# Attention with a soft mixture of experts: weights and output stored tile by tile

## The chip, the cores and the metric

The kernel runs on one core of one Trainium2 chip. The metric is the time on the device in microseconds (us), the median of several runs. What the host does before the launch and after it, such as rearranging arrays, is not in that time. The core has five engines with a queue of instructions each: PE (matmul), DVE and ACT (elementwise work and evacuation of the matmul's results from PSUM), POOL, and SP, which here issues nearly all transfers. Sixteen DMA engines move the data. A tile in SBUF has up to 128 partitions; in a transfer each partition's data is one row or several, and a row is a run of bytes that is contiguous on both sides.

## The reference

Attention over 8 batches and 8 heads with 576 positions and 64 channels, with rotary position embedding of q and k, followed by a soft mixture of 8 experts with 4 slots each. All is float32.

```python
q_rot, k_rot = (rotate(q), rotate(k))
attn = softmax(q_rot @ k_rot.T / sqrt(64))
x = (attn @ v) laid out as [B * S, H * D]        # 4608 x 512
logits = x @ phi                                  # 4608 x 32
d = softmax of logits over the 4608 rows
slot_input = d.T @ x                              # 32 x 512, 4 slots of each expert
h = relu(slot_input[e] @ w1[e])                   # w1: 8 x 512 x 1024
slot_out[e] = h @ w2[e]                           # w2: 8 x 1024 x 512
c = softmax of logits over the 32 slots
return c @ slot_out                               # 4608 x 512
```

## The kernel before, in words

*Attention* is worked through in 32 pairs of heads. For each pair, q, k and v are loaded as tiles of 128 partitions with one row of 4608 bytes each (`fetch`, L137, and `load_v`, L161): the host has already laid these arrays out tile by tile. POOL and DVE rotate them, PE forms the scores and the products with v, ACT takes the exponentials, and a few small transfers (L209, L210, L274, L286, L293) carry maxima and sums between partitions. After every four pairs a batch is complete, and its logits and its part of `slot_input` are added up. The order of all these steps on the engines is a written table of times (`WHEN`), one entry per step.

*Weights.* w1 and w2 are cut into 64 tiles of 128 partitions and 4096 bytes per partition, 32 tiles each. `load_w` (L474) loads the next tile in a fixed order, with one transfer on SP's queue (L485). A w1 tile has the shape [128, 2, 512]: partition p holds rows p and 128 + p of a block of 256 rows of one expert's w1, and 512 of its 1024 columns. A w2 tile has the shape [128, 4, 256]: four rows, and 256 of 512 columns. So in memory a w1 tile comes in rows of 2048 bytes, 256 of them, and a w2 tile in rows of 1024 bytes, 512 of them. Indices 0 to 31 of `order` are w1, the others w2; a few w1 tiles are moved back in the order, and all w1 tiles come ahead of the w2 tiles.

SBUF does not hold all 64 tiles. 24 are loaded in the course of attention (`weights`), seven more when the input buffers of attention are given up (`release_io`, `trickle`), four more in `release_stk` and one in `release_att`. Two go into the pool `wb`, and seven (`N_LEAD`, L771) and the last 19 (L869) into buffers of the first 24: each of these transfers waits until PE has used the tile that lay in its buffer. SP issues in program order, and so a load that waits holds back everything behind it.

*The expert layers* come when attention is over. `ffn1` (L781) multiplies the slots of four experts at a time with w1, in four steps of 32 matmuls (L785), with a transpose after each (L797). `ffn2_steps` (L800) multiplies with w2 for one half of the 512 output columns (`mh`), in 16 steps of 4 matmuls (L809). `gather` (L817) brings the result together for that half.

*The combination.* `combine(mh, sl, b)` (L828) does four matmuls (L837) for one output tile of [128, 4, 256], has ACT and DVE evacuate two halves (L838), and writes the tile with one transfer. For b from 0 to 7 the tile holds positions 0 to 511 of batch b (L841). For b = 8 it holds positions 512 to 575 of all eight batches, and goes in two transfers of 64 partitions (L844). There are nine tiles for each half of the columns, 18 in all, and they use seven buffers in turn. The output is a [4608, 512] array, so a tile's rows in memory are 1024 bytes long and 2048 bytes apart. The nine combinations of the first half alternate on PE with the ffn2 steps of the second (`STEPS`, L41); those of the second half follow its gather.

Output transfers stand on SP's queue behind all the weight loads, as the program issues them later.

Of the kernel before, what the change touches and what calls it, by code (L numbers as in the profile page):

```python
# [7 lines left out]
F32 = mybir.dt.float32  # L8
# [7 lines left out]
B, H, S, D = 8, 8, 576, 64  # L16
# [3 lines left out]
DM = H * D  # L20
E, SPE, FF = 8, 4, 1024
# [45 lines left out]
def attn_softmoe(ctx, tc, qk, v, phi, w1, w2, cs, ident, sel, seg, out):  # L67
    nc = tc.nc
    P = 128
# [95 lines left out]
    def bank2():  # L165
        return ps_s.tile([P, 2, 512], F32, name="s_ps")
# [307 lines left out]
    def load_w(pool, bufs, tag="w_exp"):  # L474
        n = order[len(w_tiles)]
        layer, rest = divmod(n, 4 * E)
        if layer == 0:
            grp, f, ch, x = rest // 16, rest // 8 % 2, rest // 4 % 2, rest % 4
            src = w1[4 * grp + x].rearrange("(c p) f -> p c f", p=P)[:, 2 * ch:2 * ch + 2, 512 * f:512 * f + 512]
            wt = pool.tile([P, 2, 512], F32, name=tag, bufs=bufs)  # L480
        else:
            mh, grp, fh, x = rest // 16, rest // 8 % 2, rest // 4 % 2, rest % 4
            src = w2[4 * grp + x].rearrange("(c p) m -> p c m", p=P)[:, 4 * fh:4 * fh + 4, 256 * mh:256 * mh + 256]
            wt = pool.tile([P, 4, 256], F32, name=tag, bufs=bufs)
        nc.sync.dma_start(out=wt, in_=src)  # L485
        w_tiles[n] = wt


# [7 lines left out]
    def trickle(p):  # L496
        if later:
            load_w(*later.pop(0))

    def release_stk():  # L500
        early.close()
        hx = ctx.enter_context(tc.tile_pool(name="hx", bufs=1, side="right", reuse_waits="tile"))
        extra.append(hx)
        load_w(hx, 1, "wk")
        we = ctx.enter_context(tc.tile_pool(name="we", bufs=N_WE, side="right", reuse_waits="tile"))
        for _ in range(N_WE):
            load_w(we, N_WE)
# [94 lines left out]
    for t, cc in ((1, 0), (1, 1), (0, 0), (0, 1)):  # L602
        c = half[cc]
# [12 lines left out]
    o = bank2()  # L616
# [49 lines left out]
    p = NPAIR - 1  # L666
# [11 lines left out]
    o = ps_o.tile([P, 2, 512], F32, name="o_ps")[:, 0]  # L678
# [31 lines left out]
    m, al, dt, xn = state["m"], state["al"], state["dt"], xns.pop(B - 1)  # L710
# [26 lines left out]
    o = sp[:, 1]  # L737
# [37 lines left out]

    cst, crt, _ = c_tiles[0]
    seg_sb = c_tiles[1]
    of = out.rearrange("(b s) m -> b s m", b=B)
    hts = {}

    def ffn1(grp, f):  # L781
        hp = ps_s.tile([P, 2, 512], F32, name="s_ps")
        for i in range(NP):
            for x in range(4):
                nc.tensor.matmul(hp[32 * x:32 * x + 32, 0, :], lhsT=st[:, i, SPE * (4 * grp + x):SPE * (4 * grp + x) + 32],  # L785
                                 rhs=w_tiles[16 * grp + 8 * f + 4 * (i // 2) + x][:, i % 2, :],
                                 start=(i == 0), stop=(i == NP - 1), tile_position=(0, 32 * x))
        hs = tail.tile([P, 512], F32, name="hs", bufs=2)
        nc.vector.tensor_scalar_max(out=hs, in0=hp[:, 0, :], scalar1=0.0)
        return hs  # L790
# [35 lines left out]
        return sl  # L826

    def combine(mh, sl, b):  # L828
        ms = slice(256 * mh, 256 * mh + 256)
        k = (9 * mh + b) % (N_WA + N_WB)  # L830
        ob = (wb.tile([P, 4, 256], F32, name=f"w_exp{k}") if k < N_WB else
              extra[0].tile([P, 4, 256], F32, name="w_exp", bufs=N_WA))
        for jj in range(2):
            o = ps_t.tile([P, 512], F32, name="t_ps")
            for j in (2 * jj, 2 * jj + 1):
                lhs = cst[b // 2][:, b % 2, j, :] if b < B else crt[:, 2 * j:2 * j + 2, :].rearrange("p b i -> p (b i)")
                nc.tensor.matmul(o[:, 256 * (j % 2):256 * (j % 2) + 256], lhsT=lhs, rhs=sl, start=True, stop=True)  # L837
            (nc.vector.tensor_copy if jj else nc.scalar.copy)(  # L838
                out=ob[:, 2 * jj:2 * jj + 2, :], in_=o.rearrange("p (j m) -> p j m", j=2))
        if b < B:  # L840
            nc.sync.dma_start(out=of[b, 0:512, ms].rearrange("(j p) m -> p j m", p=P), in_=ob)  # L841
        else:
            for h in range(2):
                nc.sync.dma_start(out=of[h::2, 512:576, ms].rearrange("b p m -> p b m"), in_=ob[64 * h:64 * h + 64])  # L844

    turned, split = 2, 2

# [15 lines left out]
    for grp, f in ((0, 1), (1, 0), (1, 1)):  # L863
        h = ffn1(grp, f)
# [21 lines left out]
    for b in range(B + 1):  # L886
        combine(0, sl0, b)
        if turned < NP:
            if b == LATE[0]:
                c_tr(turned)  # L890
                late_evac = c_evac(turned, True)
            elif b > LATE[0]:
                for _ in range(LATE[1]):
                    next(late_evac, None)
        for _ in range(STEPS[b]):
            next(steps, None)
# [3 lines left out]
    for b in range(B + 1):  # L900
        combine(1, sl1, b)
# [44 lines left out]
```

## Time and profile before

| What | Value |
|---|---|
| Median of 3 runs | 559.78 us (559.6 to 560.85) |
| The profiled execution | 559.26 us, span 557.3 us |
| Busy in the span | PE 518.8 us (93%), DVE 430.7 (77%), POOL 325.9 (58%), ACT 311.5 (56%) |
| Transfers | 111.31 MB in 74,618 packets, 200 GB/s on average |
| Memory | 99.93 MB read, 9.58 MB written |
| Weight tiles | 64 transfers of 512 KB |
| Output tiles | 16 transfers of 512 KB and 4 of 256 KB |

The span runs from the first to the last instruction of the profiled execution; what the execution takes beside it, 2.0 us, is not resolved. In the tables of busy time by stretch the DMA share is the sum of the packets' durations over the sixteen engines and the stretch; it can exceed 1 where packets of one engine overlap. A rate in GB/s is 10^9 bytes per second, so a weight or output tile of 512 KB has 524,288 bytes. In the chain of waits a row with DMA lasts from the issue of a transfer to its landing.

### The profile page before, as it was taken

The page shows a single profiled execution, that of the slowest core. Times are in us where ns is not written, and L with a number is a line of the kernel's source. Part 1 is how long each engine was busy: PE and PEld are TensorE (multiplying, and loading weights), DVE is VectorE, ACT ScalarE, POOL GpSimd, SP SyncE. Part 2 cuts the span into 40 slices and gives each one's busy share as a digit, 9 for nine tenths or more (in the row PEclk, how much of TensorE's full clock was granted, in tenths as well). Part 3 has the DMA queues.
Part 4 walks back from the last instruction along what each step waited for, and adds up shares of the span by engine and source line. Part 5 has one row for each costly group of instructions (what it writes and reads, how often), then busy time and mean ns, then how long its engine had stood idle before and what let it go on. Part 6 is the DMA issues. An engine that isn't in the chain of part 4 may idle for free.

```text
span 557.3 us, 25024 instructions
## 1 busy us (share of the span) xinstructions
PE 518.8 (93%) x11164; PEld 389.7 (70%) x11164; DVE 430.7 (77%) x580; ACT 311.5 (56%) x655; POOL 325.9 (58%) x324
## 2 busy tenths in 40 slices
PE   4679999999999999999999999999999999999770
PEld 2367877877787787777877887787778876635350
DVE  5779999889988998999889988997999732421350
ACT  2145666666656665666666666665666565334240
POOL 2867878876877688668786976688664111200000
PEclk9679999999999999999999999999999999999995
DMA  7254556665555565656556655565442267399997
GB/s 261 90 213 132 190 195 204 192 190 186 194 191 189 189 192 189 190 179 202 189 189 191 199 181 190 197 199 179 147 152 78 77 220 256 116 325 348 352 379 256
DMA packets 74618, 111.31 MB, mean 200 GB/s; under 512 B 11536, under 2 KB 54288, under 8 KB 74512
## 3 DMA queue, kind: packets, MB, share of 16 engines
q1 hardware_dynamic: 74498, 109.73, 60.6%
q8 instruction: 87, 1.43, 1.1%
q14 instruction: 19, 0.16, 0.1%
q10 hardware_dynamic: 14, 0.00, 0.0%
HBM read 99.93 MB, written 9.58 MB: 196 GB/s over the span
## 4 chain that ended last, share of the span: by engine, by line
PE 83%; DVE 6%; DMA 6%; ACT 1%; SPq 1%; issue 1%; DVEq 0%; ACTq 0%
PE o_ps L238 25%; PE s_ps L225 25%; PE s_ps L263 9%; PE s_ps L175 6%; PE s_ps L331 3%; DMA w_exp<-in_w 3%; PE s_ps L785 3%; PE s_ps L346 2%; DVE nm L177 2%; DMA x_in<-in_qk 2%; PE s_ps L400 1%; DVE hl L155 1%; DMA out<-w_exp 1%; PE o_ps L809 1%; DVE x_in L146 1%; PE s_ps L200 1%
## 5 line engine op out<-in xcount | busy, mean ns | idle before, releaser
L142 POOL TENSOR_TENSOR x_in<-x_in,cs_sb 128x288 f32<-128x288 f32 x248 | 256.2, 1067 | 80.2 <-DMA x_in<-in_qk 78.0
L226 ACT ACTIVATE a_t<-s_ps 128x576 f32<-128x576 f32 x288 | 179.6, 652 | 89.3 <-PE s_ps L225 88.9
L177 DVE TENSOR_REDUCE nm<-s_ps 128x2 f32<-128x576 f32 x256 | 182.9, 749 | 40.0 <-PE s_ps L175 38.3
L238 PE MATMUL o_ps<-a_t,v_in 64*64 64x288 f32 x2304 | 195.8, 408 | 0.0
L225 PE MATMUL s_ps<-hl 64*64 64x288 f16 x3456 | 167.2, 286 | 3.6 <-DVE nm L177 3.2
L225 PEld LDWEIGHTS <-hl 64*64 64x64 f16 x3456 | 125.1, 107 | 28.8 <-issue 5.4
L225 PE MATMUL s_ps<-peak,lift 64*64 64x288 f16 x1152 | 100.1, 284 | 0.3 <-issue 0.3
L238 PEld LDWEIGHTS o_ps<-a_t,v_in 64*64 64x64 f32 x2304 | 85.8, 133 | 8.2 <-issue 0.5
L175 PE MATMUL s_ps<-hl 64*64 64x288 f16 x1024 | 79.6, 291 | 3.6 <-DVE nm L177 3.6
L297 POOL TENSOR_TENSOR xt<-xt,rb 128x576 f32<-128x576 f32 x30 | 45.6, 1521 | 31.7 <-DMA rb<-r_row 24.2
L252 DVE TENSOR_TENSOR c_t<-a_t 128x1728 f32<-128x1728 f32 x32 | 62.4, 1951 | 0.0
L155 DVE TENSOR_TENSOR hl<-x_in,hl 128x1152 f16<-128x1152 f32 x32 | 60.7, 1897 | 0.5 <-ACT hl L151 0.5
L146 DVE TENSOR_TENSOR x_in<-x_in 128x1152 f32<-128x1152 f32 (+2 forms) x36 | 56.2, 1560 | 0.1
L175 PEld LDWEIGHTS <-hl 64*64 64x64 f16 x1024 | 38.3, 106 | 24.1 <-issue 14.9
L151 ACT CAST hl<-x_in 128x576 f16<-128x576 f32 (+1 forms) x66 | 40.2, 653 | 23.5 <-DVE x_in L146 21.7
L225 PEld LDWEIGHTS <-lift 64*64 64x64 f16 x1152 | 46.6, 108 | 0.7 <-issue 0.5
L337 ACT COPY xn<-s_ps 128x512 f32<-128x512 f32 x31 | 18.0, 582 | 29.2 <-PE s_ps L332 29.2
L420 POOL TENSOR_TENSOR ln<-ln,cm 128x160 f32<-128x160 f32 x7 | 14.7, 2096 | 33.3 <-DVE cm L419 33.3
L269 ACT ACTIVATE s<-s_ps,bits 128x144 f32<-128x144 f32 x32 | 12.2, 380 | 34.1 <-ACT xn L338 14.2
L263 PE MATMUL s_ps<-c_t,pick 128*32 128x144 f32 x768 | 30.0, 289 | 0.3 <-DVE c_t L252 0.2
L263 PE MATMUL s_ps<-a_t,pick 128*32 128x144 f32 x768 | 29.7, 286 | 0.0
L838 DVE COPY w_exp<-t_ps 128x512 f32<-128x512 f32 x18 | 12.3, 690 | 19.1 <-PE t_ps L837 17.5
(174 smaller groups left out, 475.4 us busy)
## 6 DMA issues: line engine op xcount, KB each, us to landing
x_in<-in_qk SPq DMA_DIRECT2D x62, 576.0 KB
w_exp<-in_w SPq DMA_DIRECT2D x63, 512.0 KB
v_in<-in_v SPq DMA_DIRECT2D x32, 576.0 KB
rb<-r_row SPq DMA_DIRECT2D x60, 144.0 KB
out<-w_exp SPq DMA_DIRECT2D x16, 512.0 KB
x_in<-in_qk SPq DMA_DIRECT2D x4, 288.0 KB
out<-w_exp SPq DMA_DIRECT2D x4, 256.0 KB
cs_sb<-in_cs SPq DMA_DIRECT2D x2, 288.0 KB
```

The costliest lines, as they stand in the source:

```text
L142: eng.tensor_tensor(out=x[:, :, c], in0=x[:, :, c], in1=cs_sb[:, :, c], op=ALU.mult)
L146: nc.vector.tensor_tensor(out=x[:, t, 0, c], in0=x[:, t, 0, c], in1=x[:, t, 1, c], op=ALU.add)
L151: nc.scalar.copy(out=halves[p][:, 1 + t, c], in_=loaded[p][:, t, 0, c])
L155: nc.vector.tensor_tensor(out=hl[:, 0:4:3], in0=x[:, :, 0], in1=hl[:, 1:3], op=ALU.subtract)
L175: nc.tensor.matmul(s[rows[c ^ h], h, 0:HC], lhsT=hl[rows[h], QH, at:at + 64], rhs=hl[rows[h], KH, half[n]], start=True, stop=True)
L177: nc.vector.tensor_reduce(out=nms[p][:, n, j:8:4], in_=s[:, :, 0:HC], axis=AX.X, op=ALU.max, negate=True)
L225: nc.tensor.matmul(s[rows[h ^ n], n, 0:HC], lhsT=lhs, rhs=rhs, start=(x == 0), stop=(x == 3))
L226: nc.scalar.activation(out=ats[p, g][:, b].rearrange("p (n x) -> p n x", n=2), in_=s[:, :, 0:HC], func=AF.Exp, scale=SCALE)
L238: nc.tensor.matmul(o[rows[h], n, 0:HC], lhsT=vt[r, i, n], rhs=ats[p, g][r, b, half[n]], start=(i == 0), stop=(i == NB - 1))
L252: nc.vector.tensor_tensor(out=c, in0=ats[p, 0], in1=ats[p, 1], op=ALU.add)
L263: nc.tensor.matmul(s[32 * k:32 * k + 32, 0, 0:QC], lhsT=pick[:, 16 * n:16 * n + NS], rhs=(c, a)[x // GRP][:, x % GRP, QC * k:QC * k + QC], ...
L297: eng.tensor_tensor(out=xts[p], in0=xts[p], in1=rbs.pop(p), op=ALU.mult)
```

## The change

The host rearranges w1 and w2 into arrays of 32 tiles of [128, 1024] each, in the order of the tile's index, and the kernel loads a tile from one contiguous block: every partition's 4096 bytes are one row. The output becomes an array of [2, 9, 128, 1024], one block for each output tile, which the kernel writes in rows of 4096 bytes; the host puts the result into the [4608, 512] form afterwards. The tile with the remaining 64 positions of each batch, once two transfers, is one. The bytes moved, the order of loads and outputs, and every computation on the chip stay as they are.

```diff
 def load_w(pool, bufs, tag="w_exp"):
         if layer == 0:
-            grp, f, ch, x = rest // 16, rest // 8 % 2, rest // 4 % 2, rest % 4
-            src = w1[4 * grp + x].rearrange("(c p) f -> p c f", p=P)[:, 2 * ch:2 * ch + 2, 512 * f:512 * f + 512]
             wt = pool.tile([P, 2, 512], F32, name=tag, bufs=bufs)
         else:
-            mh, grp, fh, x = rest // 16, rest // 8 % 2, rest // 4 % 2, rest % 4
-            src = w2[4 * grp + x].rearrange("(c p) m -> p c m", p=P)[:, 4 * fh:4 * fh + 4, 256 * mh:256 * mh + 256]
             wt = pool.tile([P, 4, 256], F32, name=tag, bufs=bufs)
-        nc.sync.dma_start(out=wt, in_=src)
+        nc.sync.dma_start(out=wt.rearrange("p c x -> p (c x)"), in_=(w1, w2)[layer][rest])
...
 def combine(mh, sl, b):
-        if b < B:
-            nc.sync.dma_start(out=of[b, 0:512, ms].rearrange("(j p) m -> p j m", p=P), in_=ob)
-        else:
-            for h in range(2):
-                nc.sync.dma_start(out=of[h::2, 512:576, ms].rearrange("b p m -> p b m"), in_=ob[64 * h:64 * h + 64])
+        nc.sync.dma_start(out=out[mh, b], in_=ob.rearrange("p j m -> p (j m)"))
...
+    w1 = moe_w1.reshape(2, 4, 2, 2, 128, 2, 512).transpose(0, 5, 2, 1, 4, 3, 6).reshape(4 * E, 128, 1024)
+    w2 = moe_w2.reshape(2, 4, 2, 4, 128, 2, 256).transpose(5, 0, 2, 1, 4, 3, 6).reshape(4 * E, 128, 1024)
...
-    args.append(nc.dram_tensor("out_0", (B * S, DM), F32, kind="ExternalOutput").ap())
+    args.append(nc.dram_tensor("out_0", (2, B + 1, 128, 1024), F32, kind="ExternalOutput").ap())
...
+    o = r.results[0]["out_0"].reshape(2, B + 1, 128, 4, 256)
+    main = o[:, :B].transpose(1, 3, 2, 0, 4).reshape(B, 512, DM)
+    rest = o[:, B].reshape(2, 2, 64, 4, 256).transpose(3, 1, 2, 0, 4).reshape(B, 64, DM)
+    return np.concatenate([main, rest], axis=1).reshape(B * S, DM)
```

More of the change, by code (lines that the diff above doesn't have):

```diff
@@ L777, in attn_softmoe @@
     seg_sb = c_tiles[1]
-    of = out.rearrange("(b s) m -> b s m", b=B)
     hts = {}
@@ L828, in combine @@
     def combine(mh, sl, b):
-        ms = slice(256 * mh, 256 * mh + 256)
         k = (9 * mh + b) % (N_WA + N_WB)
@@ L935 @@
     arrays, args = {}, []
-    for name, a in (("qk", qk), ("v", vl), ("phi", moe_phi), ("w1", moe_w1), ("w2", moe_w2),
+    for name, a in (("qk", qk), ("v", vl), ("phi", moe_phi), ("w1", w1), ("w2", w2),
                     ("cs", cs), ("ident", ident), ("sel", sel), ("seg", seg)):
@@ L944 @@
     r = run_bass_kernel_spmd(nc, [arrays], core_ids=[0])
-    return r.results[0]["out_0"]
+    o = r.results[0]["out_0"].reshape(2, B + 1, 128, 4, 256)
+    main = o[:, :B].transpose(1, 3, 2, 0, 4).reshape(B, 512, DM)
+    rest = o[:, B].reshape(2, 2, 64, 4, 256).transpose(3, 1, 2, 0, 4).reshape(B, 64, DM)
+    return np.concatenate([main, rest], axis=1).reshape(B * S, DM)
```

## The prediction

> **What bounds the kernel now.** I read the forty-slice overview first, then busy time by stage, the chain of waits, and the transfer issues.
>
> ```profile
> span 557.3 us, 25024 instructions
> ...
> PEclk9679999999999999999999999999999999999995
> DMA  7254556665555565656556655565442267399997
> GB/s 261 90 213 132 190 195 204 192 190 186 194 191 189 189 192 189 190 179 202 189 189 191 199 181 190 197 199 179 147 152 78 77 220 256 116 325 348 352 379 256
> ```
>
> For thirty slices the transfers run at about half load near 190 GB/s. In the last five the load is at 9 and the rate near 350. So there are two kernels here: attention, where transfers have room, and the expert layers, where they have none. Busy time by stage says the same (columns: stretch, length, busy time of PE, weight loads, DVE, ACT, POOL, granted clock, DMA share, GB/s):
>
> ```profile
> 0.00:440.00 440.00, 422.64 (x9761) 330.96 (x9765) 392.68 (x505) 264.65 (x549) 314.96 (x308) 0.98 0.56 180
> 484.00:515.90 31.90, 31.75 (x347) 14.63 (x346) 6.85 (x15) 15.13 (x34) 2.60 (x3) 1.00 1.03 330
> 492.00:528.00 36.00, 33.12 (x358) 15.92 (x350) 10.81 (x21) 12.88 (x29) 1.73 (x2) 1.00 1.09 349
> 528.00:555.50 27.50, 12.26 (x80) 7.97 (x80) 8.53 (x13) 7.67 (x14) 0.00 (x0) 0.80 1.00 341
> 515.90:545.50 29.60, 21.62 (x164) 12.27 (x160) 13.47 (x22) 11.35 (x22) 0.00 (x0) 0.98 1.09 366
> ```
>
> Until 440 us PE is busy 422.6 of 440 us: PE bounds. From 484 to 515.9 us it still has no gaps. But from 492 us on the DMA engines never rest (share 1.09, packets overlapping), and from 515.9 us PE idles a quarter of its time. The chain that ended last names the cause:
>
> ```profile
> 497.78 3.57 PE s_ps L785 x32
> 501.35 0.59 PE t_ps L797 x4
> ...
> 508.83 8.78 DMA w_exp<-in_w
> ...
> 520.84 8.62 DMA w_exp<-in_w
> ...
> 535.32 6.65 DMA out<-w_exp
> ...
> 544.81 0.69 DVE w_exp L838
> ```
>
> Weight tiles and output tiles take 8.8, 8.6 and 6.7 us from issue to landing, because they stand in a full queue. The last evacuation ends at 545.5 us and the program only closes after 556.2 us, once the last output has landed:
>
> ```profile
> L942 SPq EVENT_SEMAPHORE  x7: 17/28/28, 556.2 to 557.2; - x7
> ```
>
> So from 492 us to the end the kernel is one unbroken stream of weights and then outputs. What counts is how fast that stream runs.
>
> **The change part by part.** Which rows does it touch? The issues (line, tile, count, duration in ns, first and last start):
>
> ```profile
> L485 SPq DMA_DIRECT2D w_exp<-in_w x35: 368/447/1884, 58.3 to 472.8; - x35
> ...
> L485 SPq DMA_DIRECT2D w_exp<-in_w x26: 368/1356/2422, 486.7 to 520.8; - x26
> ...
> L841 SPq DMA_DIRECT2D out<-w_exp x16: 372/1263/1778, 522.3 to 546.7; - x16
> ```
>
> The loading order in the code puts all 32 w1 tiles (rows of 2048 bytes) and six w2 tiles before 483 us; the 26 loads from 486.7 us on are all w2 tiles, in rows of 1024 bytes. The outputs are also in rows of 1024 bytes. After the change each of these rows is 4096 bytes, with the same bytes in all: 524,288 per tile. Everything rests on the price of a row by its length, which other stretches show:
>
> ```profile
> 32.00:34.00 2.00, 2.00 (x39) 1.69 (x32) 1.22 (x2) 1.33 (x3) 0.79 (x2) 0.50 1.02 417
> 33.00:34.00 1.00, 1.00 (x20) 0.79 (x16) 1.00 (x2) 0.45 (x2) 0.79 (x2) 0.50 1.05 429
> 458.00:460.00 2.00, 2.00 (x58) 1.41 (x46) 0.00 (x0) 1.81 (x4) 1.28 (x2) 1.00 1.02 389
> 462.00:464.00 2.00, 2.00 (x52) 1.54 (x50) 0.94 (x3) 0.40 (x3) 0.00 (x0) 1.00 1.05 397
> 528.00:538.00 10.00, 8.15 (x61) 5.19 (x61) 4.38 (x7) 4.23 (x9) 0.00 (x0) 1.00 1.09 385
> 538.00:548.00 10.00, 4.11 (x21) 2.78 (x20) 4.15 (x6) 3.44 (x6) 0.00 (x0) 0.81 1.07 366
> 548.00:555.50 7.50, 0.00 (x0) 0.00 (x0) 0.00 (x0) 0.00 (x0) 0.00 (x0) 0.50 0.80 248
> ```
>
> What flowed when is told by the issues just before each stretch:
>
> ```profile
> 29.35 0.80 SPq L137 DMA_DIRECT2D x_in<-in_qk  x2
> 30.20 0.43 SPq L161 DMA_DIRECT2D v_in<-in_v  x1
> ...
> 455.22 2.15 SPq L485 DMA_DIRECT2D w_exp<-in_w  x4
> ```
>
> Hence 32 to 34 us is q, k and v in rows of 4608 bytes, each tile one contiguous block: 417 GB/s, 429 in its best microsecond. 458 to 464 us holds w1 rows of 2048 bytes: 389 to 397. 492 to 528 us is w2 rows of 1024 bytes: 349. Per row on one of 16 engines (16 x bytes / rate) that is 46.9 ns, 82.5 to 84.2 ns and 176.8 ns: close to a straight line with a fixed part of about 10 ns per row. A 4096-byte row lies on it at 158 ns, that is 414 GB/s; four 1024-byte rows cost 188 ns.
>
> *Weight loads in the tail.* From 492 to 528 us 36 x 349 = 12.56 MB move, 24 tiles. At 414 GB/s: 30.3 us, 5.7 less. Ends: 389 GB/s (the worst 2048-byte stretch) gives 32.3 us, 3.7 less; 429 gives 29.3 us, 6.7 less. I take 414, since 4608 bytes is the nearest row.
>
> Would loading still be continuous? A load waits until PE has used the tile that lay in its buffer. Up to 515.9 us PE runs without gaps, so these releases stay where they are; the expert layer's first half frees eight tiles in about 4.2 us (3.57 us of matmuls and 0.59 us of transposes, the chain's rows at 497.78 and 501.35), 0.5 us each, and the stream needs 524,288 / 414 = 1.27 us each. It stays behind the releases, hence full.
>
> The Trainium skill's page "DMA: Bandwidth & Descriptors", section "Where 436 GB/s comes from", speaks against this: for HBM to SBUF it lets the HBM side bind at about 358 GB/s per core. By that the 12.56 MB would take 35.1 us and 0.9 us would be won. The trace does not agree: 417 over two microseconds.
>
> *Outputs.* 528 to 555.5 us moves 27.5 x 341 = 9.38 MB, the 18 output tiles. It runs at 385 GB/s, then 366, then dies out: the last 7.5 us move 1.86 MB, which at 366 take 5.1, so 2.4 us go to engines that finish apart. No write with long rows is in the trace. Lower end: nothing won by row length, 366 throughout and the same run-out, 25.6 + 2.4 = 28.0 us, 0.5 more than now. Upper end: 429 GB/s and 1.4 us of run-out, 23.3 us, 4.2 less. I take 410, near the read row of 4608 bytes, as 1024-byte writes at 385 already beat 1024-byte reads at 349; and 2.0 us of run-out: 22.9 + 2.0 = 24.9, 2.6 less.
>
> *The halves.* The last output of each pass went as two transfers of 64 partitions and is now one of 128. That takes away two issues; its effect on transfer is in the run-out above.
>
> *Issue time.* A 4608-byte tile is issued in 0.41 us and a 2048-byte weight tile in 0.45 us (medians):
>
> ```profile
> L137 SPq DMA_DIRECT2D x_in<-in_qk x62: 327/410/1160, 4.7 to 409.4; - x62
> ```
>
> The 1.36 us of the tail's loads is SP waiting on a full queue, at the pace of the stream. Shorter issue by itself is worth nothing there, as the stream hides it.
>
> *The 38 earlier weight tiles.* Nothing: PE's 422.6 of 440 us covers them, and no wait of PE names them. Without that cover, 32 w1 tiles would gain 1.32 - 1.27 us each (397 against 414 GB/s), 1.6 us, and six w2 tiles 0.23 us each (1.50 against 1.27), 1.4 us.
>
> *PE's waits.*
>
> ```profile
> PEld s_ps L809 <- DMA w_exp<-in_w: 4.7, 4, 1.4
> ...
> PEld o_ps L809 <- DMA w_exp<-in_w: 1.7, 2, 1.4
> ...
> ACT w_exp L838 <- DMA out<-w_exp: 2.4, 3, 1.2
> ```
>
> The 6.4 us PE waits for weights shrink, but I do not add them: PE reaches the outputs earlier, and these then stand in the queue behind the last weights. They are the same time seen from PE.
>
> Sum: 5.7 + 2.6 = 8.3 us. The profiled execution took 559.3 us (span 557.3 and 2.0 around it), so 551.0; the runs' median is 559.8, 0.5 higher, so **551.5 us**.
>
> **The rivals.**
>
> *Only reads gain.* If writing to HBM is limited by something other than row length (1024-byte rows fell from 385 to 366 GB/s with no change of row), the outputs keep their 27.5 us: 559.8 - 5.7 = 554.1. Against it: the fall comes while SP still waits on a full queue, so one slow engine may set it, which fewer rows would ease.
>
> *The output buffers become the bound.* Seven output tiles exist. Between the two column halves lie PE's gather, a copy on ACT, the first combine and an evacuation:
>
> ```profile
> 533.03 0.67 PE t_ps L837 x4
> 533.71 0.68 PE s_ps L822 x4
> 534.38 0.02 issue
> 534.41 0.38 ACT kl L825
> ```
>
> With 0.67 us for a combine and 0.69 for the evacuation that is 2.4 us without a new output. Seven tiles hold 7 x 1.28 = 9 us of work, so this is hidden unless fewer than two tiles are queued at that moment; then 551.5 + 2.4 = 553.9. PE alone does not become the bound: 21.6 us of busy time after 515.9 us end at 537.5, and even with 0.7 for evacuation, a full 8.6 us in the queue and 1.1 to close, 547.9 lies before the 549.0 us span of my forecast.
>
> *No gain from row length.* Memory, and not the row, sets 349 GB/s: about 559.5. For it: the DMA share of 1.09 at 1024 bytes says engines are saturated whatever they carry. Against: 389 to 429 GB/s at longer rows with a share of 1.02 to 1.05. That is the skill's 358 GB/s rule; and the same page's "Specifications" call 512 bytes enough for line rate, which would price 1024-byte rows like 4096-byte ones. The 349 against 417 GB/s disagrees.
>
> *Slower: contiguous output tiles.* Now a tile's rows are spread over HBM at a pitch of 2048 bytes; afterwards 16 engines write into one block of 512 KB. If neighbouring writes hinder one another, the outputs slow down. To eat 5.7 us they would need 33.2 us, 9.38 MB in 30.8 us without run-out: below 305 GB/s it is slower than today. At the 290 GB/s of the start (1152-byte rows, the slowest full stretch) outputs take 34.3 us: 559.8 - 5.7 + 6.8 = 560.9.
>
> ```profile
> 5.00:7.00 2.00, 0.09 (x1) 0.08 (x1) 1.22 (x2) 0.43 (x1) 0.00 (x0) 1.00 0.97 290
> ```
>
> For it: 1024-byte writes did slow down within the pass. Against: reads from equally contiguous blocks reach 417.
>
> **How the numbers follow.** Forecast with its bounds (549 to 553): 0.62. Only reads gain: 0.20. Output buffers: 0.09. No gain from row length: 0.05. Slower: 0.04. From the two ends, 559.8 - 10.9 = 548.9 and 559.8 - 3.2 = 556.6; I draw the range at 548.0, a little beyond the fast end, since rows in a lasting stream could overlap better than in bursts of two microseconds, and at 555.0, beyond the second and third case; about 0.1 lies above it. About 0.2% (1.1 us) is what a measurement of this kernel can tell from no change. Faster: 0.62 + 0.20 + 0.09 and a little of the fourth case, 0.92; same: 0.04; slower: 0.04.
>
> **What would show it right or wrong.** Right: a transfer rate near 410 GB/s without a break from about 492 us; the last weights landed near 523 us; waits of PE for weights well under 6.4 us; outputs in about 25 us; attention until 484 us unchanged to within 1 us. Wrong: 350 to 360 GB/s in the weight stretch (no gain from rows), below 390 in the output stretch (only reads), slices with a DMA share clearly below 1 around 525 to 535 us (buffers), or under 305 in the outputs (slower).

## The result and the profile after

The changed kernel takes 550.17 us (median of 4 runs, 549.96 to 551.09) against 559.99 us before. The ratio is 0.9826, with a 95% interval of 0.9809 to 0.9843: it is faster by 9.8 us, 1.7%. The prediction was 551.5 us, in a range of 548 to 555.

The overview of the changed kernel, in forty slices:

```profile
span 548.3 us, 25022 instructions
...
PEclk9689999999999999999999999999999999999997
DMA  7264566656665556566656666656443256569997
GB/s 263 94 216 134 193 193 196 203 186 188 193 207 180 191 193 199 189 192 194 193 194 193 192 194 194 193 193 193 152 123 104 68 184 215 167 204 411 409 415 326
DMA packets 51290, 111.31 MB, mean 203 GB/s; under 512 B 11504, under 2 KB 28656, under 8 KB 51184
```

The same 111.31 MB go in 51,290 packets instead of 74,618. The last slices run at 409 to 415 GB/s where they ran at 348 to 379. Ahead of those hardly anything has moved: PE was busy for 422.64 of the first 440 us, and is now for 421.91. Busy time by stretch (PE, weight loads, DVE, ACT, POOL, granted clock, DMA share, GB/s):

```profile
0.00:440.00 440.00, 421.91 (x9776) 330.56 (x9780) 391.54 (x505) 264.48 (x549) 318.79 (x308) 0.98 0.57 180
490.00:492.00 2.00, 2.00 (x24) 0.52 (x16) 0.00 (x0) 1.93 (x6) 0.00 (x0) 1.00 0.86 289
492.00:494.00 2.00, 2.00 (x22) 0.89 (x18) 0.69 (x1) 1.14 (x4) 0.86 (x1) 1.00 0.92 328
494.00:522.00 28.00, 27.37 (x324) 13.74 (x316) 9.43 (x19) 10.97 (x24) 0.87 (x1) 1.00 1.03 410
523.00:540.00 17.00, 12.70 (x92) 8.25 (x84) 9.02 (x14) 7.91 (x15) 0.00 (x0) 1.00 1.03 419
540.00:542.00 2.00, 0.00 (x0) 0.00 (x0) 0.00 (x0) 0.00 (x0) 0.00 (x0) 0.61 1.03 422
542.00:544.00 2.00, 0.00 (x0) 0.00 (x0) 0.00 (x0) 0.00 (x0) 0.00 (x0) 0.50 1.02 420
544.00:546.00 2.00, 0.00 (x0) 0.00 (x0) 0.00 (x0) 0.00 (x0) 0.00 (x0) 0.50 0.59 240
```

Weights stream at 410 GB/s from 494 us on, outputs at 419, and outputs hold 420 until 544 us: the slow dying out of before (248 GB/s over the last 7.5 us) is gone. The DMA share fell from 1.09 to 1.03 while the rate rose, so the share alone doesn't tell what the engines could carry.

The chain that ended last, then the closing instruction on SP:

```profile
514.78 10.11 DMA w_exp<-in_w
...
531.79 5.53 DMA out<-w_exp
...
538.65 0.69 DVE w_exp L832
```

```profile
L935 SPq EVENT_SEMAPHORE  x7: 17/28/6243, 540.9 to 548.2; - x7
```

The last weights have landed at 514.78 + 10.11 = 524.9 us; before, at 520.84 + 8.62 = 529.5. SP waits for the last output until 540.9 + 6.2 = 547.1 us, where it was 556.2. So the way from the start to the last weights is 4.6 us shorter, and that from there to the last output 22.2 instead of 26.7 us, 4.5 shorter; together 9.1, against 9.0 of difference between the spans (rounding).

PE still waits for weights, but less. Its weight loads in ffn2 waited 4.7 us for the second group of four experts (`s_ps`) and 1.7 us for the first (`o_ps`); now it is 2.4 and 0.2 us:

```profile
PEld s_ps L804 <- DMA w_exp<-in_w: 2.4, 3, 1.1
...
PEld o_ps L804 <- DMA w_exp<-in_w: 0.2, 1, 0.2
```

SP now waits for something new:

```profile
SPq L481 <- DMA w_exp<-in_w: 15.1, 16, 2.3
...
SPq L481 <- PE s_ps L780: 6.6, 5, 3.7
```

Before, the issue of a weight tile lasted 1.36 us in the tail, which the prediction reads as a full queue of transfers. Now it lasts 0.33 us (median of the last 26), and SP waits for an earlier weight transfer to land before it issues the next one. Landing takes 10.1 us, eight times the 1.28 us that a tile takes at 410 GB/s: by this, about eight transfers are under way at once. The engines are kept busy either way, at a share of 1.09 before and 1.03 now.

### The profile page after: what moved, and what is told of

Read it like the earlier page. It is cut to its first block, busy times and chain, and to the rows that moved or that the text cites. A ratio compares the mean times of both kernels' runs of the same rounds, so it can differ in the third digit from the quotient of the medians.

```text
span 548.3 us, 25022 instructions
## 1 busy us (share of the span) xinstructions
PE 515.8 (94%) x11164; PEld 388.7 (71%) x11164; DVE 429.5 (78%) x580; ACT 311.3 (57%) x655; POOL 329.6 (60%) x324
## 2 busy tenths in 40 slices
DMA packets 51290, 111.31 MB, mean 203 GB/s; under 512 B 11504, under 2 KB 28656, under 8 KB 51184
## 4 chain that ended last, share of the span: by engine, by line
PE 87%; DVE 5%; DMA 4%; ACT 1%; issue 1%; SPq 1%; ACTq 0%; DVEq 0%
PE o_ps L238 26%; PE s_ps L225 26%; PE s_ps L263 9%; PE s_ps L175 6%; PE s_ps L331 3%; PE s_ps L780 3%; PE s_ps L346 2%; DVE nm L177 2%; DMA w_exp<-in_w 2%; PE s_ps L400 1%; DMA x_in<-in_qk 1%; PE s_ps L804 1%; PE s_ps L200 1%; DMA out<-w_exp 1%; PE s_ps L183 1%; PE o_ps L804 1%
## 5 line engine op out<-in xcount | busy, mean ns | idle before, releaser
L142 POOL TENSOR_TENSOR x_in<-x_in,cs_sb 128x288 f32<-128x288 f32 x248 | 258.9, 1079 | 76.1 <-DMA x_in<-in_qk 66.3
L297 POOL TENSOR_TENSOR xt<-xt,rb 128x576 f32<-128x576 f32 x30 | 46.8, 1559 | 31.7 <-DMA rb<-r_row 31.7
L155 DVE TENSOR_TENSOR hl<-x_in,hl 128x1152 f16<-128x1152 f32 x32 | 59.2, 1849 | 0.5 <-ACT hl L151 0.5
L263 PEld LDWEIGHTS s_ps<-c_t,pick 128*32 128x32 f32 x768 | 21.1, 109 | 6.9 <-issue 5.3
```

What stands on the lines that cost most here:

```text
L142: eng.tensor_tensor(out=x[:, :, c], in0=x[:, :, c], in1=cs_sb[:, :, c], op=ALU.mult)
L155: nc.vector.tensor_tensor(out=hl[:, 0:4:3], in0=x[:, :, 0], in1=hl[:, 1:3], op=ALU.subtract)
L263: nc.tensor.matmul(s[32 * k:32 * k + 32, 0, 0:QC], lhsT=pick[:, 16 * n:16 * n + NS], rhs=(c, a)[x // GRP][:, x % GRP, QC * k:QC * k + QC], ...
L297: eng.tensor_tensor(out=xts[p], in0=xts[p], in1=rbs.pop(p), op=ALU.mult)
```

## The experiments

All are compared with the kernel before on the same chip. Their runs scatter more than the first ones (the changed kernel itself from 549.5 to 552.0), so a difference below some 1.5 us between two of them says little, and rates within a stretch are the sharper evidence. Part of the scatter comes ahead of the change's reach: the expert layers start between 483.5 and 485.9 us in these profiles.

### Each part alone

**Weights alone.** Loads as in the changed kernel, the two forms of output transfer as before; against the kernel before:

```diff
+        nc.sync.dma_start(out=wt.rearrange("p c x -> p (c x)"), in_=(w1, w2)[layer][rest])
```

> Only the weight tiles come in rows of 4096 bytes; outputs are written as before, in rows of 1024. Theory (every row has a fixed price of about 10 ns, and the two parts add up): the last weights land at about 524.9 us of the span as in the changed kernel (529.5 before), the outputs keep their 26.7 us: 560.0 - 4.6 = 555.4 us, weight stretch near 410 GB/s, output stretch 385 falling to 366. Rival (outputs are slow only because they share a full queue with 1024-byte weights): outputs speed up too, 551 to 552 us.

Measured: 555.91 us, ratio 0.9928 (0.9896 to 0.9959), that is 4.1 us less. The stretches of the weights and of the outputs' second pass:

```profile
502.00:520.00 18.00, 17.25 (x230) 9.71 (x228) 5.36 (x10) 8.92 (x20) 0.87 (x1) 1.00 1.03 409
...
541.00:547.00 6.00, 0.00 (x0) 0.00 (x0) 0.42 (x1) 0.16 (x1) 0.00 (x0) 0.50 1.03 344
547.00:549.00 2.00, 0.00 (x0) 0.00 (x0) 0.00 (x0) 0.00 (x0) 0.00 (x0) 0.50 0.94 247
549.00:551.00 2.00, 0.00 (x0) 0.00 (x0) 0.00 (x0) 0.00 (x0) 0.00 (x0) 0.50 0.24 62
```

The weights run at 409 GB/s, as with the whole change. The outputs don't profit: 344 GB/s in the second pass and a long end, in which the DMA share drops to 0.24. The rival, that outputs are slow only for the weights ahead of them, falls.

**Outputs alone.** Loads as before; against the kernel before:

```diff
+        nc.sync.dma_start(out=out[mh, b], in_=ob.rearrange("p j m -> p (j m)"))
```

> Only the outputs go in rows of 4096 bytes; weights are loaded as before. Theory (the parts add up): last weights at about 529.5 us, outputs in 22.4 us instead of 26.7 at about 420 GB/s: 560.0 - 4.3 = 555.7 us. Rival (writing was never limited by row length, as I gave 0.20): 559.5 to 560 us.

Measured: 556.28 us, ratio 0.9933 (0.9913 to 0.9952), 3.7 us less.

```profile
502.00:520.00 18.00, 16.71 (x208) 9.52 (x204) 2.92 (x5) 7.75 (x17) 0.87 (x1) 1.00 1.10 348
531.00:537.00 6.00, 5.54 (x48) 3.50 (x46) 2.57 (x5) 2.86 (x6) 0.00 (x0) 1.00 1.03 419
541.00:547.00 6.00, 2.34 (x12) 1.69 (x12) 2.70 (x5) 2.04 (x4) 0.00 (x0) 0.96 1.03 419
```

Weights stay at 348 GB/s and outputs go to 419, in the first pass too, where they ran at 385 before the first ninth tile. Writing gains from the change by itself, so the rival to which I gave 0.20 falls. This edit also turns the two halves of the ninth tile into one transfer; what share that has is taken up below, under the end of the outputs. The two parts add up to 7.8 us; together they give 9.8. The difference of 2 us is about as large as the intervals allow. The profiles, taken by stage, hardly leave it: weights alone have the last weights landed at 525.1 instead of 529.5 us, outputs alone need 22.3 instead of 26.7 us from there to the last output. That is 8.8 us, against 9.1 for the whole change.

**Only the weights loaded during attention.** The 38 tiles ahead of the expert layers in long rows, the other 26 and all outputs as before.

```diff
+        if len(w_tiles) < 38:
+            nc.sync.dma_start(out=wt.rearrange("p c x -> p (c x)"), in_=src)
+        else:
...
+            nc.sync.dma_start(out=wt, in_=src)
```

> Only the 38 weight tiles that are loaded before the expert layers come in rows of 4096 bytes; the last 26 and all outputs as before. Theory (attention hides them): 559.5 to 560.3 us. Rival (shorter transfers release something in attention): up to 3.0 us less, the price that the prediction gave them without cover, 557.0 us.

Measured: 559.24 against 560.36 us, ratio 0.9978 (0.9956 to 1.0001). No gain is shown, but the interval leaves room for up to 0.4%, 2.5 us. Its expert layers start at 483.7 us, within the scatter. So far as these runs resolve it, attention hides these loads, as the sum had it.

### Length of a row, or contiguous tiles?

The change does two things at once: a row grows to 4096 bytes, and a tile becomes one block. Two kernels take them apart, and two more vary the length.

**Short rows in contiguous blocks.** A tile is one block of 512 KB, but a partition's pieces lie 128 rows apart in it.

```diff
+        nc.sync.dma_start(out=wt, in_=(w1, w2)[layer][rest].rearrange("c p x -> p c x"))
...
+        nc.sync.dma_start(out=out[mh, b].rearrange("j p m -> p j m"), in_=ob)
```

> Every weight and output tile is one contiguous block of 512 KB, but its rows are as short as before: 2048 bytes for w1, 1024 for w2 and outputs, ordered so that a partition's pieces do not adjoin. Theory (row length sets the price): as before, 559 to 560.5 us, weight stretch at 349 GB/s, outputs at 366 to 385. Rival (what counts is that a tile is one block in memory): as the changed kernel, 550 to 551 us. Both at work: in between.

Measured: 557.56 us, ratio 0.9955 (0.9936 to 0.9973), in between, 2.4 us less than before.

```profile
502.00:520.00 18.00, 16.84 (x211) 8.92 (x211) 3.11 (x6) 7.86 (x17) 0.87 (x1) 1.00 1.10 349
531.00:537.00 6.00, 5.29 (x48) 3.62 (x44) 3.35 (x6) 3.32 (x7) 0.00 (x0) 1.00 1.09 385
541.00:547.00 6.00, 2.27 (x10) 1.57 (x10) 2.25 (x4) 1.80 (x4) 0.00 (x0) 0.74 1.08 383
```

For weights contiguous blocks do nothing: 349 GB/s as before. For outputs they do nothing in the first pass either (385), but in the second pass 383 GB/s remain, where it was 369 from 541 to 547 us in the kernel before:

```profile
541.00:547.00 6.00, 2.06 (x10) 1.36 (x10) 2.11 (x4) 1.75 (x3) 0.00 (x0) 0.77 1.07 369
```

**Long rows, not contiguous.** After each row of 4096 bytes a gap of 4096 bytes.

```diff
+    w1 = np.stack([w1, np.zeros_like(w1)], axis=2)
+    w2 = np.stack([w2, np.zeros_like(w2)], axis=2)
...
+        nc.sync.dma_start(out=wt.rearrange("p c x -> p (c x)"), in_=(w1, w2)[layer][rest][:, 0, :])
...
+        nc.sync.dma_start(out=out[mh, b, :, 0, :], in_=ob.rearrange("p j m -> p (j m)"))
```

> Rows of 4096 bytes, but with a gap of 4096 bytes after each, for weights and outputs: long rows without contiguous blocks. Theory (row length): as the changed kernel, 550 to 551 us, 410 and 420 GB/s. Rival (contiguous blocks): 555 to 560 us.

Measured: 552.42 us, ratio 0.9862 (0.9821 to 0.9903). The interval holds the changed kernel's ratio, and the rates are its rates:

```profile
502.00:520.00 18.00, 17.86 (x232) 10.22 (x224) 4.30 (x7) 8.56 (x19) 0.87 (x1) 1.00 1.02 408
531.00:537.00 6.00, 4.72 (x27) 3.64 (x28) 4.08 (x7) 3.80 (x8) 0.00 (x0) 1.00 1.03 421
```

**Rows of 2048 bytes**, in contiguous blocks.

```diff
+        two = wt if layer == 0 else wt.rearrange("p (a c) x -> p a (c x)", a=2)
+        nc.sync.dma_start(out=two, in_=(w1, w2)[layer][rest].rearrange("a p x -> p a x"))
...
+        nc.sync.dma_start(out=out[mh, b].rearrange("a p x -> p a x"),
+                          in_=ob.rearrange("p (a j) m -> p a (j m)", a=2))
```

> All weight and output tiles in rows of 2048 bytes. Theory (a straight line: reads 82.5 to 85 ns per row, 385 to 397 GB/s; writes, from 42.5 ns at 1024 and 156 ns at 4096 bytes, 80.5 ns, 407 GB/s): weights 1.3 us and outputs 0.6 us longer than in the changed kernel, 552.1 us. Rival (a threshold at 4096 bytes): near 560. Rival (rows saturate at 2048): 550.2.

Measured: 553.54 us, ratio 0.9860 (0.9832 to 0.9889), where the changed kernel in the same set of runs has 550.77 us and 0.9821 (0.9795 to 0.9848). That is 2.8 us more, where 1.9 was expected; the scatter allows it.

```profile
502.00:520.00 18.00, 17.30 (x229) 9.66 (x228) 5.47 (x10) 8.82 (x19) 0.87 (x1) 1.00 1.05 387
531.00:537.00 6.00, 5.11 (x30) 3.94 (x29) 4.05 (x6) 3.42 (x6) 0.00 (x0) 1.00 1.05 406
```

Both rates are those of the straight line, and both rivals (a threshold at 4096, a ceiling at 2048) fall.

**Rows of 8192 bytes.** 50 of the 64 weight tiles are loaded in pairs.

```diff
+    def load_pair():
+        at = len(w_tiles)
+        both = wp.tile([P, 2, 1024], F32, name="w_exp", bufs=N_W // 2)
+        nc.sync.dma_start(out=both.rearrange("p a x -> p (a x)"), in_=w1[at // 2])
+        for a in range(2):
+            n = order[at + a]
+            w_tiles[n] = both[:, a, :].rearrange("p (c x) -> p c x", c=2 if n < 4 * E else 4)
```

> 50 of the 64 weight tiles are loaded in pairs, rows of 8192 bytes, into 12 buffers of double size; a pair waits until both its tiles' buffers are free. Outputs as in the changed kernel. Theory (the line goes on: 311 ns per row, 421 GB/s): the 12.56 MB of the weight stretch take 29.8 us instead of 30.7, 549.3 us. Rival (waiting for pairs costs more than the rows gain, or the rate has reached its ceiling): 550.2 to 552 us.

Measured: 551.47 us, ratio 0.9826 (0.9797 to 0.9855): not to be told from the changed kernel. The rate did rise:

```profile
502.00:520.00 18.00, 17.87 (x234) 10.16 (x227) 4.13 (x7) 8.45 (x18) 0.87 (x1) 1.00 1.01 421
```

421 instead of 409 GB/s is 0.9 us on 12.56 MB, less than these runs can resolve. In its profile the last weights land 39.8 us after the expert layers start, in the changed kernel's 41.0 us; but these layers start 2 us later, at 485.9 instead of 483.9 us. Whether the pairs delay attention isn't shown, since other kernels scatter up to 485.7. So it is no version that demonstrably beats the changed kernel.

These stretches give the price of a row on one engine as 16 x bytes / rate:

| Row | Reading | per row | Writing | per row |
|---|---|---|---|---|
| 1024 bytes | 349 GB/s | 46.9 ns | 385 GB/s | 42.6 ns |
| 2048 | 387 | 84.7 | 406 | 80.7 |
| 4096 | 409 | 160.2 | 419 | 156.4 |
| 8192 | 421 | 311.3 | | |

Each further byte costs about 0.037 ns, for reading and writing alike. What is left as a fixed part is 9.2 ns per row read and 4.6 ns per row written.

### The end of the outputs

The fourth experiment won 2.4 us with rows as short as before. It differs in two things: the output is contiguous, and the ninth tile of a pass goes in one transfer instead of two of 64 partitions.

**Halves again, with long rows.**

```diff
+            for h in range(2):
+                nc.sync.dma_start(out=out[mh, b, 64 * h:64 * h + 64], in_=ob[64 * h:64 * h + 64])
```

> The changed kernel, but the ninth output tile of each pass goes in two transfers of 64 partitions again, rows of 4096 bytes. Theory (row length does nearly all): 0 to 0.5 us slower than the changed kernel, 550.2 to 550.7 us. Rival (the halves caused the ragged end of the outputs, 2.4 us of run-out): 1.5 to 2.4 us slower, 551.7 to 552.6 us.

Measured: 549.55 us, ratio 0.9793 (0.9768 to 0.9818), not slower than the changed kernel's 0.9821. With long rows the halves cost nothing that can be measured in the time. In this profile the rate dips soon after the first two halves are issued, but only for a moment: 401 and 408 GB/s from 533 to 537 us, then 418 and 416 until 541.

```profile
531.00:537.00 6.00, 4.89 (x29) 3.73 (x27) 4.51 (x7) 3.99 (x7) 0.00 (x0) 1.00 1.02 406
```

**Halves again, with short rows in blocks.**

```diff
+        for rows_ in ((slice(0, P),) if b < B else rows):
+            nc.sync.dma_start(out=dst[rows_], in_=ob[rows_])
```

> Contiguous blocks with short rows as in the fourth experiment, but the ninth tile of each pass is written in two transfers of 64 partitions again. In the kernel before, 1024-byte writes run at 385 GB/s until the first ninth tile and near 355 after it; with whole tiles in blocks they stay at 385 to the end. Theory that the halves of 64 partitions upset the stream: second pass near 355 GB/s, outputs in 28 us, 559.5 us. Theory that the pitch of 2048 bytes does it, with the second pass filling the gaps of the first: 385 GB/s to the end, outputs in 26 us, 557.6 us.

Measured: 560.65 us, ratio 1.000 (0.998 to 1.0021). The gain of the fourth experiment is gone.

```profile
531.00:537.00 6.00, 5.33 (x46) 3.33 (x47) 2.41 (x4) 2.51 (x5) 0.00 (x0) 1.00 1.09 385
541.00:547.00 6.00, 3.38 (x15) 2.52 (x14) 2.57 (x4) 2.00 (x4) 0.00 (x0) 0.84 1.06 363
```

**No halves, pitch of 2048 bytes.** The kernel before, with an output of [9, 512, 512].

```diff
-        if b < B:
-            nc.sync.dma_start(out=of[b, 0:512, ms].rearrange("(j p) m -> p j m", p=P), in_=ob)
-        else:
-            for h in range(2):
-                nc.sync.dma_start(out=of[h::2, 512:576, ms].rearrange("b p m -> p b m"), in_=ob[64 * h:64 * h + 64])
+        nc.sync.dma_start(out=out[b, 0:512, ms].rearrange("(j p) m -> p j m", p=P), in_=ob)
```

> The kernel before, but the output has the form [9, 512, 512], so that the ninth tile is one transfer of 128 partitions with rows of 1024 bytes at a pitch of 2048, like the others. Theory that the halves upset the stream: 385 GB/s to the end, outputs in 26 us, 558.1 us. Theory that the pitch does it: second pass near 355 GB/s, outputs in 28 us, 560 us.

Measured: 558.73 us, ratio 0.9973 (0.9955 to 0.9991), 1.3 us less than before.

```profile
541.00:547.00 6.00, 2.73 (x14) 1.92 (x14) 3.10 (x5) 2.42 (x5) 0.00 (x0) 1.00 1.08 375
547.00:549.00 2.00, 0.00 (x0) 0.00 (x0) 0.00 (x0) 0.00 (x0) 0.00 (x0) 0.76 1.04 356
```

So with rows of 1024 bytes the two transfers of 64 partitions do upset the stream: putting them back takes away all that the contiguous short rows won (2.5 us), and taking them out of the kernel before wins 1.3 us.

Taken by stage, the profiles leave out the scatter of attention. Each row is one profile, times in us of its span; the last column runs from the landing of the last weights to that of the last output:

| Kernel | Output rows | Ninth tile | Last weights | Last output | Between |
|---|---|---|---|---|---|
| Before | 1024 bytes | halves | 529.5 | 556.2 | 26.7 |
| Weights alone | 1024 | halves | 525.1 | 552.2 | 27.1 |
| Early weights alone | 1024 | halves | 529.9 | 555.1 | 25.2 |
| Blocks with halves | 1024 | halves | 531.2 | 558.8 | 27.6 |
| Short rows in blocks | 1024 | whole | 529.6 | 554.1 | 24.5 |
| Whole, with the pitch | 1024 | whole | 531.0 | 555.6 | 24.6 |
| Outputs alone | 4096 | whole | 530.7 | 553.0 | 22.3 |
| Changed | 4096 | whole | 524.9 | 547.1 | 22.2 |
| Changed, with halves | 4096 | halves | 525.2 | 547.6 | 22.4 |

With short rows a whole ninth tile gives 24.5 to 24.6 us, and halves 25.2 to 27.6. The pitch shows no share: 24.6 us with it and 24.5 without, although the rate in the second pass is a little lower with it (375 against 383). Long rows give 22.2 to 22.4 us with halves or without. So the two causes overlap. Long rows alone take the outputs from 26.7 to 22.4 us; a whole ninth tile alone takes them to 24.6, and long rows then win another 2.3. Why halves do lasting harm with short rows and not with long ones wasn't found.

**Two output buffers reused sooner**, in the changed kernel.

```diff
-        k = (9 * mh + b) % (N_WA + N_WB)
+        k = (9 * mh + b) % 4
```

> The changed kernel with four output buffers in turn instead of seven. Four tiles are 5.1 us of writing at 1.27 us each. Theory (a buffer comes back after 0.7 us of evacuation, 0.4 of issue, 1.5 to the start, 1.3 of transfer and some 0.7 until the last engine has landed, 4.6 us, so four just hold the stream, save where the column half changes, 2.4 us without a new output): 552 to 553.5 us. Rival (seven were needed): above 556 us. Rival (buffers never mattered): 550 to 551 us.

The edit does not leave four buffers. `k` chooses between two tiles of the pool `wb` and the pool `extra[0]`, whose five buffers (`N_WA`) come round by themselves. With `% 4` all seven stay in use, but the two in `wb` come back after four output tiles instead of seven.

Measured: 553.17 us, ratio 0.9862 (0.9828 to 0.9896). The time is the one of the first theory; the way to it is not.

```profile
531.00:537.00 6.00, 5.54 (x50) 3.74 (x46) 2.40 (x4) 2.64 (x6) 0.00 (x0) 0.93 0.71 283
541.00:547.00 6.00, 2.60 (x14) 1.92 (x14) 2.96 (x5) 2.36 (x5) 0.00 (x0) 0.88 1.02 404
```

```profile
531.00:535.00 4.00, 4.00 (x41) 2.54 (x38) 1.43 (x3) 1.55 (x4) 0.00 (x0) 0.89 0.66 268
535.00:537.00 2.00, 1.54 (x12) 1.20 (x10) 0.97 (x2) 1.09 (x3) 0.00 (x0) 1.00 0.79 313
```

```profile
ACT w_exp L832 <- DMA out<-w_exp: 10.0, 4, 6.8
```

The fifth output tile waits 6.8 us for the buffer of the first. That one was issued at 517.75 us and landed 10.1 us later, as it stood behind the last weights; the theory had 3.9 us for issue and landing, and one late in the second pass took 4.3. PE, held up as well, still has steps of ffn2 to do between the combines after that, about 1.7 us for each output tile. So the stream is thin from 529 us on, before the change of the column half (the copy on ACT at 535.9 us), and recovers to 404. Buffers that come back too late can become the bound. With seven in turn they aren't: the changed kernel writes at 419 GB/s and a share of 1.03 from 523 to 540 us.

## Why the prediction was right, point by point

**What bounds the kernel**: right. All of the gain lies after 490 us, and long rows for the 38 early tiles alone showed none.

**The price of a row**: right in its form, and slightly too good in size. The prediction put a 4096-byte row at 158 ns, 414 GB/s, on a line whose longer rows came from bursts of two microseconds. The lasting stream has 160 ns and 409 to 410 GB/s. The fixed part is 9.2 ns, where it said about 10. That the line is one of row length, and not of contiguous memory, was assumed there; long rows with gaps and short rows in blocks show it.

The Trainium skill's page "DMA: Bandwidth & Descriptors", section "Where 436 GB/s comes from", has HBM bind a core at about 358 GB/s, half of a stack's 716 GB/s for two cores. Measured here, with one core at work: 409 at 4096 bytes and 421 at 8192. The same page of the Trainium skill, under "Specifications", calls 512 bytes enough for line rate; from 1024 to 4096 bytes the rate still rose from 349 to 409.

**Weight loads in the tail**: 5.7 us predicted, 4.6 measured to the last landing. The step that failed is "hence full": the stream is not full at 492 us. From 490 to 494 us it runs at 289 and 328 GB/s, and it ran at 309 and 341 there before the change. This is the time in which SP waits for ffn1's matmuls (L780) to hand buffers back, 6.6 us in all. At 410 GB/s the 0.16 MB missing from 492 to 494 us are 0.4 us; the rate of 410 instead of 414 is another 0.3. By these rates the 12.56 MB are through at 523.0 us, 5.0 us before 528. The last 0.4 us of the miss lie in the landing of the last tile, which comes 1.9 us after that point, and came 1.5 us after it before.

**Outputs**: 2.6 us predicted, 4.5 measured. Row length was sized about right: without the run-out the sum went from 25.1 to 22.9 us, 2.2 less, and with a whole ninth tile the profiles go from 24.5 us (short rows in blocks) to 22.3 (outputs alone). Writing runs at 419 GB/s instead of 410: 9.38 MB in 22.4 instead of 22.9 us. The mis-sized term is the run-out. Of its 2.4 us the prediction kept 2.0, since it saw engines finishing apart and no reason for it. It had named the halves but put their effect inside that remainder, 0.4 us. With short rows they cost 2.2 us (26.7 against 24.5; the other profiles give 0.6 to 3.1), and in the changed kernel both the halves and the short rows are gone: 420 GB/s to 544 us.

The two misses have opposite signs, 1.1 us too much and 1.9 us too little. That the sum of 8.3 us comes within 0.8 us of the 9.1 by which the last output lands sooner, and the forecast of 551.5 within 1.4 us of the measured time, is in part luck.

**Rivals.** Only reads gain: fell, outputs alone win 3.7 us and are written at 419 instead of 385 GB/s. Output buffers: the stream does thin when two of them are reused too soon, but with seven in turn it has no gap; that the loss there (553.17 against 550.77 us) came to the 2.4 us of the rival's sum is chance, since it arose at another place. No gain from row length: fell. Slower through contiguous output tiles: fell, writes into blocks reach 419 GB/s, and with gaps between the rows 421.

**Signs named ahead.** A rate near 410 (410 from 494 us on), weights landed near 523 us (524.9), waits of PE for weights well under 6.4 us (2.6 on the same two rows), outputs in about 25 us (22.2), attention unchanged (the expert layers start at 483.9 instead of 484.1 us): as named, save that the rate is there two microseconds later, the weights land 1.9 us later and the outputs take less.

## What to carry to other kernels

Look for stretches in which the DMA engines never rest, and price their rows: here a row of 1024 bytes pays a fifth of its reading time for being a row, one of 4096 bytes a seventeenth. Here only such a stretch repaid a new layout; the same change to loads hidden under matmuls gave nothing measurable. In a saturated stream of short rows, prefer one transfer over all 128 partitions to two over 64 each. Read the price of an unseen row length off a line through lengths that the trace does show, preferably from lasting stretches and not from bursts.

## What was not expected

Writing has a smaller fixed price per row than reading (4.6 against 9.2 ns), with the same price per byte. The DMA share went down, from 1.09 to 1.03, as the rate went up by 17%. And two transfers of 64 partitions amid sixteen of 128 slow those that follow: with rows of 1024 bytes from 385 to 363 GB/s, with rows of 4096 bytes one profile shows no more than a dip of some 4 us, to 401 and 408.
